# Regrouping the steps of an attention pair by kind, with one more pair in flight

## Chip, core and metric

The kernel runs on one core of one Trainium2 chip. The metric is the device time of an execution in microseconds (us); three runs of the kernel before have a median of 559.45 us (558.18 to 561.83).

The engines are named as in the profile: PE is TensorE's matmuls, PEld its weight loads, DVE is VectorE, ACT is ScalarE, POOL is GpSimd and SP is the queue that issues most DMAs. L491 is line 491 of the kernel.

## What is computed

The reference is blockwise causal attention followed by a mixture of experts with one expert per token:

```python
# attention: B, H, S, D = 8, 8, 576, 64; blocks of 64
scores = scale * q @ k.T                       # per batch and head
scores = where(pos_q // 64 >= pos_k // 64, scores, -1e9)
scores = scores - max(scores, axis=-1)
attn = exp(scores);  attn = attn / (sum(attn) + 1e-9)
x = (attn @ v), heads side by side             # [B, S, 512]
# experts: E = 8, F = 1024
logits = x @ w_gate;  local = sigmoid(x @ w_local)
for each batch, for s in order:                # a scan over the tokens
    e = argmax(logits[s]) if s == 0 or local[s] < 0.5 else e of token s - 1
    out[s] = softmax(logits[s])[e] * (relu(x[s] @ w1[e]) @ w2[e])
```

## The kernel before

**Pairs.** Attention works on 32 pairs of heads (NPR = 32; four pairs are one batch). A pair's queries and keys come in by DMA in their natural layout (`load_qk`, tile `natb`, two buffers), are turned by eight 128x128 transposes into the PSUM tile `ps_t` (L742), and are copied by ACT into `plb` (L747, L748; two buffers). The last 64 tokens, the tail, go through one more transpose (L775) and two small copies (L792, L793). From `plb` DVE makes rounded copies `kh` (keys, L749) and `qd` (queries laid out block-diagonally, L751); POOL adds their tails (L795, L797).

**Maxima.** `top` computes each query block's scores roughly from `kh` and `qd` in three jobs (L464, L470), and DVE takes the row maxima (L474 to L480). `shift` lets POOL spread their negatives into `diag`.

**Scores.** The exact scores are made in four segments (`SEGS`). `products` (L491) multiplies keys and queries in fp32, the two heads on separate halves of TensorE's rows; `less` (L499) adds the negative maxima from `diag` into the same PSUM tile `ps_s`; `expo` (L509) lets ACT write the exponentials to `prob`, and POOL clears the masked corners (L514).

**Products with V.** `av` (L522, L530) multiplies `prob` by V with a column of ones; `norm` (L438, L439) divides by the sums on DVE. `turn_x` and `turn_x_tail` (L536, L542) transpose the result x for the gate, `store_x` writes it to DRAM as bf16, and after every second pair `gate_sums` (L555, L561) adds up the gate's logits.

**PSUM.** The jobs' tiles, `ps_t` and `ps_s` share one pool of two buffers (`ps_sp`, 2 banks each); one more tile of two banks (`ps_mp`) serves jobs 1 and 2; `g0` and `g1` have a bank each.

**The loop.** The program's order on every engine is the order written out by hand. In pass `it` four pairs are in work: a = it + 2 (turned, maxima of jobs 0 and 1), c = it + 1 (maxima of job 2, then scores), e = it (products with V) and x = it - 1 (turned for the gate, stored). The order within a pass is: loads; job 2 of c and its `shift`; norm and store of x; Q/K transposes of a; score segments 0 and 1 of c, interleaved; turning x and the tail of a; jobs 0 and 1 of a; tail of x; part of e's products with V; score segments 2 and 3 of c; the rest of `shift`; the expert weights' DMA for one slice (`load_weights`); the rest of e's products with V; gate sums.

**Routing work** is hung into passes by a table `plan` with places "begin", "turn", "mid" and "end". In passes 9, 17 and 25 `fresh` and `fresh_b` find each token's own best expert (with one ACT exponential, L162) and `to_rows` lays the choice out in rows; one pass later `scan_rows` scans them; two passes later `chosen_ps` and `chosen` fetch the result and `ranks_ps` starts the ranks; three passes later `ranks`, `ranks_b` and `shares` finish. Passes 29 and 30 plan the experts' tiles (`plan1`, `high`, `low`, `inverse`).

After pass 31 the experts' phase runs 38 tiles of 128 tokens, with the last quarter's routing between them. It uses the memory of `natb` and `plb` for the current expert's first weights (`w1c`).

Of the kernel before, what the change touches and what calls it, by code (L numbers as in the profile page):

```python
# [16 lines left out]
def kernel(  # L17
# [11 lines left out]
    nc = tc.nc  # L29
    F32 = mybir.dt.float32  # L30
# [15 lines left out]
    P = 128  # L46
# [43 lines left out]
    def rt(shape, dt, name):  # L90
# [46 lines left out]
    natb = rt([P, 2, 9, 2, D], F32, "natb")  # L137
    plb = rt([P, 2, 2 * S + 64], F32, "plb")
    w1c = [t[:, 0:WE] for t in (natb.rearrange("p z t h d -> p (z t h d)").bitcast(BF16),
                                plb.rearrange("p z n -> p (z n)").bitcast(BF16))]  # L140
# [233 lines left out]
    with tc.manual_schedule():  # L374
# [25 lines left out]
        def load_qk(i, eng=nc.sync):  # L400

            b, hp = divmod(i, HP)
            t = natb[:, i % 2]
            for w, src in enumerate((q, k)):
                s = src[b, 2 * hp:2 * hp + 2]
                for h in range(2):
                    eng.dma_start(out=t[:, 4 * w:4 * w + 4, h, :],
                                  in_=s[h, :512].rearrange("(so si) d -> si so d", si=128))
                eng.dma_start(out=t[64 * w:64 * w + 64, 8],
                              in_=s[:, 512:S].rearrange("h p d -> p h d"))  # L410
            nats[i] = t

# [90 lines left out]
        def seg_tile():  # L503
            return ps_sp.tile([P, 2, 512], F32, tag="s", name="ps_s")

# [39 lines left out]
        def keep_x(x, g0, g1):  # L545
            xTs[x] = o_p.tile([P, S], F32, tag="xT", name="xT")
            nc.scalar.copy(xTs[x][:, 0:512], g0)
            nc.scalar.copy(xTs[x][:, 512:576], g1[:, 256:320])
# [104 lines left out]


        load_qk(0)
        load_qk(1, nc.scalar)
        nc.sync.dma_start(out=wgl[:, :, :E],
# [5 lines left out]
        def scr_f(a, n):  # L663
# [8 lines left out]
        nat_bf = natb.rearrange("p z t h d -> p (z t h d)").bitcast(BF16)  # L672
        ohl1 = nat_bf[:, 0:n1 * P].rearrange("p (c t) -> p c t", t=P)
        rhs1 = nat_bf[:, n1 * P:n1 * (P + 2 * NT1)].rearrange("p (c j t) -> p c j t",
                                                              j=2, t=NT1)
# [4 lines left out]
        tmpt1 = scr_f(2312, NT1 * E)[0:1].rearrange("p (t e) -> p t e", e=E)  # L680

# [34 lines left out]
        for it in range(-2, NPR):  # L716
            a, c, e, x = it + 2, it + 1, it, it - 1
            on_a, on_c, on_e, on_x = (0 <= y < NPR for y in (a, c, e, x))
            if it >= -1 and 1 <= a and a + 1 < NPR:
                load_qk(a + 1)  # L720
            if on_c:
                load_v(c)

            if on_c:
                top(c, 2, ps_mp)
                shift(c, 2, 2)
                shift(c, 8, 1)
            if on_x:
                norm(x, g0_b, 0, 6)
                store_x(x)  # L730
# [6 lines left out]
            if on_a:  # L737
                nat = nats[a]
                ps = ps_sp.tile([P, 2, 512], F32, tag="s", name="ps_t")
                for w in (1, 0):  # L740
                    for t in range(4):
                        nc.tensor.transpose(ps[:, w, 128 * t:128 * t + 128],  # L742
                                            nat[:, 4 * w + t].rearrange("p h d -> p (h d)"),
                                            id_f)
                pl = pls[a] = plb[:, a % 2]
                mxs[a] = o_p.tile([P, 9], F32, tag="mx", name="mx")
                nc.scalar.copy(pl[:, S:S + 512], ps[:, 1, :])  # L747
                nc.scalar.copy(pl[:, 0:512], ps[:, 0, :])  # L748
                nc.vector.tensor_copy(kh[:, 0:512], pl[:, S:S + 512])  # L749
# [5 lines left out]
            if on_c:  # L755
                ps0, ps1 = seg_tile(), seg_tile()
                products(c, ps0, 0, 0)
                products(c, ps1, 1, 0)
                less(ps0, 0, 0)
                products(c, ps0, 0, 1)  # L760
                less(ps0, 0, 1)
                expo(c, ps0, 0)
                less(ps1, 1, 0)
                products(c, ps1, 1, 1)
                less(ps1, 1, 1)
                expo(c, ps1, 1)

            b_done = (x - 1) // HP if on_x and x >= 1 and (x - 1) % HP == HP - 1 else None
            if on_a or on_e or on_x:
                g1 = g_tile(1)  # L770
            if on_x:
                g0 = g_tile(0)
                turn_x(x, g0)
            if on_a:
                nc.tensor.transpose(g1[:, 384:512],  # L775
                                    nat[:, 8].rearrange("p h d -> p (h d)"), id_f)
            if b_done is not None:
                turn_sums(b_done, g1)
            run(it, "turn", g1)
            if on_a:  # L780
                top(a, 0, ps_sp)
                top(a, 1, ps_mp)
            if on_x:
                turn_x_tail(x, g1)
            if on_e:
                xs[e] = o_p.tile([P, 9, D], F32, tag="x", name="x", bufs=1)
                av(e, g1, 4)
                av(e, g1, 3)
            if on_x:
                keep_x(x, g0, g1)  # L790
            if on_a:
                nc.scalar.copy(pl[:, 512:576], g1[:, 384:448])  # L792
                nc.scalar.copy(pl[:, 2 * S - 64:2 * S + 64].rearrange("p (a t) -> p a t", a=2),  # L793
                               g1[:, None, 448:512].to_broadcast([P, 2, 64]))
# [5 lines left out]
            if on_e:  # L800
                norm(e, g1, 6, 3)
            run(it, "mid", g1)

            if on_c:
                for z in (2, 3):
                    ps = seg_tile()
                    products(c, ps, z, 0)
                    less(ps, z, 0)
                    expo(c, ps, z)
            if on_a:  # L810
                shift(a, 4, 4)
                shift(a, 0, 2)
# [11 lines left out]

            if on_e:
                g0_b = g_tile(0)
                for m in (2, 1, 0):
                    av(e, g0_b, m)
# [30 lines left out]
        def results():  # L859
            cur[0], cur[1] = g_tile(0), g_tile(1)  # L860
            turn_x(x, cur[0])
            turn_x_tail(x, cur[1])
            keep_x(x, cur[0], cur[1])
# [116 lines left out]
```

## Time and profile before

| | us |
|---|---|
| three runs: median (lowest, highest) | 559.45 (558.18, 561.83) |
| the profiled execution | 556.25 |
| its span, first to last instruction | 554.4 |
| start to pass 0 | 26.56 |
| passes 0 to 30 | 362.43 |
| pass 31 and the experts' phase | 165.41 |
| a plain pass, up to its gate sums (it 14) | 11.16 |
| the same with its gate sums, which every second pass has | 11.94 |

The profile is of one execution, with 1.85 us outside its span. Passes are told apart in the PE timeline by the job of four matmuls (L470 x4) that opens each, since everything on PE comes in program order. Rows there are merged: "x4" is four instructions of one line in a row, with the start of the first. A matmul's end is modelled, so the distance between starts says more than the length. Mean granted TensorE clock is 0.994.

### The profile page before, as it was taken

Reading aid. Unit: us, or ns where it says so; the run is one execution under the profiler, and the core shown is the slowest. Engines: PE = TensorE matmul, PEld = TensorE weight load, DVE = VectorE, ACT = ScalarE, POOL = GpSimd, SP = SyncE. Lnnn points to the kernel's source line nnn. Section 1 sums busy time; section 2 is a strip of 40 time slices with the busy share of each in tenths; the row PEclk is TensorE's granted clock in tenths of the full one; section 3 lists DMA queues with packets and bytes.
Section 4 is the critical chain, followed back from the end, with each engine's and each line's share of the span. In section 5 each row is a group of like instructions: output and inputs, shape, how many; then the busy total and the mean of one; then the engine's idle time right before and its main releaser. Section 6 shows DMA issues by size and latency. Waiting matters only on the chain.

```text
span 554.4 us, 18510 instructions
## 1 busy us (share of the span) xinstructions
PE 517.1 (93%) x7327; PEld 398.9 (72%) x7327; DVE 334.3 (60%) x756; ACT 248.3 (45%) x487; POOL 254.6 (46%) x510
## 2 busy tenths in 40 slices
PE   2899999999999999999999999999899989999991
PEld 2567777778777777876777777787777767777770
DVE  2565555655759656566855466699557885444440
ACT  1345444454544454444444444544354544454450
POOL 2343343433453433353333435334668766766752
PEclk9999999999999999999999999999999999999997
DMA  6377766885578977468987638964523323323321
GB/s 121 85 127 140 142 139 124 139 150 115 104 136 146 163 146 141 86 116 148 165 158 128 135 71 138 173 109 74 110 79 105 118 90 108 117 89 111 105 89 52
DMA packets 161060, 66.44 MB, mean 120 GB/s; under 512 B 145076, under 2 KB 153292, under 8 KB 160972
## 3 DMA queue, kind: packets, MB, share of 16 engines
q0 software_dynamic: 17760, 31.79, 28.9%
q1 hardware_dynamic: 140812, 32.83, 28.9%
q8 instruction: 61, 1.00, 0.8%
q10 hardware_dynamic: 2400, 0.59, 0.6%
q14 instruction: 27, 0.22, 0.2%
HBM read 67.48 MB, written 15.00 MB: 149 GB/s over the span
## 4 chain that ended last, share of the span: by engine, by line
PE 72%; DVE 10%; issue 5%; ACT 4%; DMA 3%; POOL 2%; SPq 1%; POOLq 0%; DVEq 0%; ACTq 0%
PE ps_s L491 13%; PE g L530 12%; PE ps_h L628 10%; PE ps_o L640 9%; PE ps_m L470 7%; DVE mx L480 5%; PE ps_m L464 4%; PE ps_s L499 3%; ACT plb L748 3%; PE g L522 3%; PE g L536 3%; PE ps_t L742 2%; PE g L555 1%; PE g L542 1%; PE ps_x L613 1%
## 5 line engine op out<-in xcount | busy, mean ns | idle before, releaser
L491 PE MATMUL ps_s<-plb 64*128 64x320 f32 (+4 forms) x768 | 130.0, 419 | 6.6 <-ACT plb L748 6.6
L509 ACT ACTIVATE prob<-ps_s 128x1024 f32<-128x1024 f32 (+2 forms) x128 | 100.3, 835 | 60.6 <-PE ps_s L499 49.4
L491 PEld LDWEIGHTS ps_s<-plb 64*128 64x128 f32 x768 | 62.9, 187 | 48.2 <-ACT plb L748 29.0
L530 PEld LDWEIGHTS g<-vt,prob 128*64 128x64 f32 x2560 | 79.9, 138 | 9.8 <-issue 9.8
L530 PE MATMUL g<-vt,prob 128*64 128x65 f32 x2560 | 86.9, 223 | 0.0
L480 DVE TENSOR_REDUCE mx<-ps_m 128x1 f32<-128x576 f32 (+2 forms) x96 | 43.3, 506 | 67.7 <-PE ps_m L470 67.7
L483 POOL TENSOR_TENSOR diag<-negi,mx 128x128 bf16<-128x128 f32 (+2 forms) x128 | 52.1, 424 | 59.8 <-DVE rs L438 25.5
L640 PE MATMUL ps_o<-w_bf,hT 128*128 x304 | 71.7, 379 | 0.0
L474 DVE TENSOR_REDUCE mx<-ps_m 128x2 f32<-128x1024 f32 x32 | 39.1, 1223 | 48.1 <-PE ps_m L470 48.1
L514 POOL MEMSET prob<- 64x128 f32 x128 | 23.8, 199 | 89.8 <-ACT prob L509 85.3
L470 PE MATMUL ps_m<-kh,qd 128*128 128x512 f32 (+5 forms) x224 | 56.2, 336 | 2.1 <-DVE mx L477 2.1
L632 ACT ACTIVATE hT<-ps_h 128x512 bf16<-128x512 f32 x76 | 45.4, 598 | 26.3 <-PE ps_h L628 25.9
L499 PE MATMUL ps_s<-diag,ones 64*128 64x320 bf16 (+4 forms) x384 | 48.5, 274 | 1.1 <-POOL diag L483 1.1
L644 ACT ACTIVATE o_sb<-ps_o,share 128x512 f32<-128x512 f32 x38 | 26.1, 688 | 51.1 <-PE ps_o L640 43.0
L640 PEld LDWEIGHTS <-hT 128*128 128x128 bf16 x304 | 28.3, 98 | 27.3
L795 POOL CAST kh<-plb 128x64 fp32r<-128x64 f32 x32 | 7.6, 237 | 84.9 <-issue 76.4
L747 ACT COPY plb<-ps_t 128x512 f32<-128x512 f32 x32 | 18.8, 586 | 62.0 <-PE ps_t L742 62.0
L617 DVE COPY scr<-ps_x 128x512 bf16<-128x512 bf16 x38 | 16.1, 424 | 49.8 <-PE ps_x L613 49.5
L470 PEld LDWEIGHTS ps_m<-kh,qd 128*128 128x128 f32 x224 | 38.1, 193 | 7.6 <-issue 1.8
L742 PE MATMUL ps_t<-id_f,natb 128*128 128x128 f32 x256 | 35.0, 282 | 8.0 <-DMA natb<-in_k_dram 8.0
L628 PEld LDWEIGHTS <-plb 128*128 128x128 bf16 x608 | 35.4, 98 | 5.8 <-DVE plb L608 1.7
L751 DVE CAST qd<-plb 64x512 fp32r<-64x512 f32 x64 | 39.0, 609 | 0.6
(194 smaller groups left out, 865.5 us busy)
## 6 DMA issues: line engine op xcount, KB each, us to landing
w_bf<-in_moe_w_dram POOLq DMA_DIRECT2D x32, 512.0 KB, 6.0
vt<-in_v_dram SPq DMA_DIRECT2D x64, 128.0 KB
natb<-in_q_dram SPq DMA_DIRECT2D x62, 128.0 KB
natb<-in_k_dram SPq DMA_DIRECT2D x62, 128.0 KB
x_rows<-xb SPq DMA_DIRECT2D x32, 128.0 KB
vt<-in_v_dram SPq DMA_DIRECT2D x32, 32.0 KB
x_rows<-xb SPq DMA_DIRECT2D x64, 8.0 KB
natb<-in_q_dram SPq DMA_DIRECT2D x31, 32.0 KB
```

The lines of the kernel that those rows point to most:

```text
L470: nc.tensor.matmul(flat[:, c + k0:c + k0 + nn], lhsT=qd[:, b, :], rhs=kh[:, k0:k0 + nn], start=True, stop=True)
L474: nc.vector.reduce_max(mx[:, 6:8], ps, axis=AX)
L480: nc.vector.reduce_max(mx[:, b:b + 1], flat[:, c:c + n], axis=AX)
L483: nc.gpsimd.tensor_tensor(diag[:, s0:s0 + n, :], negi[:, None, :].to_broadcast([P, n, 64]), mxs[i][:, s0:s0 + n, None].to_broadcast([P, n, ...
L491: nc.tensor.matmul(ps[:, h, c:c + n], lhsT=pls[i][rows(h), S + 128 * j:S + 128 * j + 128], rhs=pls[i][rows(h), a:a + n], start=True, stop= ...
L499: nc.tensor.matmul(ps[:, h, c:c + n], lhsT=ones[rows(h), :], rhs=diag[rows(h), a // 64:(a + n) // 64, :], start=False, stop=True)
L509: nc.scalar.activation(p[:, :, SEG0[s]:SEG0[s] + w], ps[:, :, 0:w], func=AF.Exp, scale=scale_attn)
L530: nc.tensor.matmul(g[rows(e), o + 65 * h:o + 65 * h + 65], lhsT=p[:, h, c:c + 64], rhs=t[:, j, h, :], start=(j == 0), stop=(j == m))
L628: nc.tensor.matmul(ps_h[:, f, :], lhsT=w[:, ko * F + fo * P:ko * F + fo * P + P], rhs=xb[:, ko * P:(ko + 1) * P], start=(ko == 0), stop=(k ...
L632: nc.scalar.activation(hT[:, half * 4:half * 4 + 4, :], ps_h, func=AF.Relu)
L640: nc.tensor.matmul(ps_o, lhsT=hT[:, fo, :], rhs=w2_bf[:, bass.ds(woff + fo * Dm, Dm)], start=(fo == 0), stop=(fo == FO - 1))
L742: nc.tensor.transpose(ps[:, w, 128 * t:128 * t + 128], nat[:, 4 * w + t].rearrange("p h d -> p (h d)"), id_f)
```

## The change

The steps of a pass are regrouped, and a fifth pair is in work: r = it + 3 is turned, a = it + 2 has all three maxima jobs, c = it + 1 all four score segments (in the order 3, 2, 0, 1, one after the other), e and x are as before. The loop starts at -3. The order on PE is: maxima of a; turning x; Q/K transposes and tail of r; scores of c; tail of x; all products with V of e; gate sums.

Turned queries and keys have three buffers. Natural queries and keys have one, which is loaded again once the pair in it has been turned (pair 1's natural data sits in the third turned buffer, which is still unused then). `load_qk` is split: the four large loads, then the two tails (`load_tails`). The bf16 copy of x (`xb`) has one buffer instead of two. On SP the order in a pass is now: the stores of x, the loads of Q/K, the loads of V. On ACT the copy of turned x, the copies of turned Q/K with their tails, and the gate's sums come ahead of all four exponentials.

Routing work moves with it: what was in "mid" is mostly in "turn", ahead of the scores on ACT and DVE; `chosen_ps` has a new place "ahead"; `shares` comes a pass later; `low` in pass 30 is one operation in "begin".

```diff
-    natb = rt([P, 2, 9, 2, D], F32, "natb")
-    plb = rt([P, 2, 2 * S + 64], F32, "plb")
...
+    PLW, NAW = 2 * S + 64, 9 * 2 * D
+    qkb = rt([P, NAW + 3 * PLW], F32, "qkb")
+    plb = [qkb[:, NAW + PLW * i:NAW + PLW * i + PLW] for i in range(3)]
+    qk_bf = qkb.bitcast(BF16)
+    w1c = [qk_bf[:, z:z + WE] for z in (0, 2 * (NAW + PLW))]
...
-            t = natb[:, i % 2]
+            z = NAW + 2 * PLW if i == 1 else 0
+            t = qkb[:, z:z + NAW].rearrange("p (t h d) -> p t h d", h=2, d=D)
...
+        def load_tails(i, eng=nc.sync):
+            b, hp = divmod(i, HP)
+            for w, src in enumerate((q, k)):
+                eng.dma_start(out=nats[i][64 * w:64 * w + 64, 8],
+                              in_=src[b, 2 * hp:2 * hp + 2, 512:S].rearrange("h p d -> p h d"))
...
-            xb = o_p.tile([P, 9, D], BF16, tag="xb", name="xb")
+            xb = o_p.tile([P, 9, D], BF16, tag="xb", name="xb", bufs=1)
...
-            at(i0, "mid", lambda ps, g=g: fresh(g))
-            at(i0, "mid", lambda ps, g=g: fresh_b(g))
+            at(i0, "turn", lambda ps, g=g: fresh(g))
+            at(i0, "turn", lambda ps, g=g: fresh_b(g))
...
-            at(i0 + 1, "mid", lambda ps, g=g: scan_rows(g, buf))
-            at(i0 + 2, "turn", lambda ps, g=g: chosen_ps(g, ps, buf))
-            at(i0 + 2, "mid", lambda ps, g=g: chosen(g, ps))
+            at(i0 + 1, "turn", lambda ps, g=g: scan_rows(g, buf))
+            at(i0 + 2, "ahead", lambda ps, g=g: chosen_ps(g, ps, buf))
+            at(i0 + 2, "turn", lambda ps, g=g: chosen(g, ps))
...
-            at(i0 + 3, "turn", lambda ps, g=g: shares(g))
-            at(i0 + 3, "mid", lambda ps, g=g: ranks(g))
+            at(i0 + 3, "turn", lambda ps, g=g: ranks(g))
             at(i0 + 3, "mid", lambda ps, g=g: ranks_b(g))
+            at(i0 + 4, "turn", lambda ps, g=g: shares(g))
...
-        at(30, "turn", lambda ps: low(ohl1[:, 0:GC, :], 0, GC))
-        at(30, "mid", lambda ps: low(ohl1[:, GC:n1, :], GC, n1 - GC))
+        at(30, "begin", lambda ps: low(ohl1, 0, n1))
```

The loop body after the change:

```python
for it in range(-3, NPR):
    r, a, c, e, x = it + 3, it + 2, it + 1, it, it - 1
    if on_x:
        norm(x, g0_b, 0, 6)
    run(it, "begin", ge)
    ...
    for job, pool in enumerate((ps_sp, ps_sp, ps_mp)):
        if on_a:
            top(a, job, pool)
    ...
    if on_x:
        g0 = g_tile(0)
        turn_x(x, g0)
        store_x(x)
        nc.scalar.copy(xT_of(x)[:, 0:512], g0)
    if on_r:
        ...
        nxt = {0: 2, 1: None}.get(r, r + 1 if r + 1 < NPR else None)
        if nxt is not None:
            load_qk(nxt)
            load_tails(nxt)
    if on_c:
        load_v(c)
    if b_done is not None:
        turn_sums(b_done, g1)
    run(it, "ahead", g1)
    if on_r:
        ...
    if b_done is not None:
        keep_sums(b_done, g1)
    run(it, "turn", g1)
    if on_c:
        for z in (3, 2, 0, 1):
            ps = ps_sp.tile([P, 2, 512], F32, tag="s", name="ps_s")
            for part in range(len(SEGS[z])):
                products(c, ps, z, part)
                less(ps, z, part)
            expo(c, ps, z)
    if on_a:
        shift(a, 0, 5)
        shift(a, 5, 4)
    if -1 <= it < NPR - 1:
        load_weights(it + 1)
    ...
    if on_x:
        turn_x_tail(x, g1)
    if on_e:
        av(e, g1, 4)
        av(e, g1, 3)
    if on_x:
        nc.scalar.copy(xT_of(x)[:, 512:576], g1[:, 256:320])
    if on_e:
        norm(e, g1, 6, 3)
        run(it, "mid", g1)
        g0_b = g_tile(0)
        for m in (2, 1, 0):
            av(e, g0_b, m)
    ...
```

More of the change, by code (lines that the diff above doesn't have):

```diff
@@ L543, in turn_x_tail, with xT_of @@
                                  rhs=id_f[:, rows(h)], start=True, stop=True)
[L545 to L548, printed above, removed]
+        def xT_of(x):
+            if x not in xTs:
+                xTs[x] = o_p.tile([P, S], F32, tag="xT", name="xT")
+            return xTs[x]
         def gate_sums(x, gl):
@@ L671 @@
         n1 = 3 * GC
[L672 to L675, printed above, removed]
+        ohl1 = qk_bf[:, 0:n1 * P].rearrange("p (c t) -> p c t", t=P)
+        rhs1 = qk_bf[:, n1 * P:n1 * (P + 2 * NT1)].rearrange("p (c j t) -> p c j t",
+                                                             j=2, t=NT1)
         ohh1 = scr[:, 0:n1 * NT1].rearrange("p (c t) -> p c t", t=NT1)
@@ L715 @@
         ge = None
[L716 to L727, printed above, removed]
+        for it in range(-3, NPR):
+            r, a, c, e, x = it + 3, it + 2, it + 1, it, it - 1
+            on_r, on_a, on_c, on_e, on_x = (0 <= y < NPR for y in (r, a, c, e, x))
             if on_x:
                 norm(x, g0_b, 0, 6)
-                store_x(x)
             run(it, "begin", ge)
@@ L736 @@
                 first(1)
-            if on_a:
-                nat = nats[a]
+            for job, pool in enumerate((ps_sp, ps_sp, ps_mp)):
+                if on_a:
+                    top(a, job, pool)
+            b_done = (x - 1) // HP if on_x and x >= 1 and (x - 1) % HP == HP - 1 else None
+            if on_r or on_e or on_x:
+                g1 = g_tile(1)
+            if on_x:
+                g0 = g_tile(0)
+                turn_x(x, g0)
+                store_x(x)
+                nc.scalar.copy(xT_of(x)[:, 0:512], g0)
+            if on_r:
+                nat, pl = nats[r], plb[r % 3]
+                pls[r] = pl
+                mxs[r] = o_p.tile([P, 9], F32, tag="mx", name="mx")
                 ps = ps_sp.tile([P, 2, 512], F32, tag="s", name="ps_t")
@@ L753 @@
                         pl[rows(h), 0:512].rearrange("p (b t) -> p b t", t=64))
[L755 to L794, printed above, removed]
                 nc.gpsimd.tensor_copy(kh[:, 512:576], pl[:, 2 * S - 64:2 * S])
@@ L799 @@
                 keep_sums(b_done, g1)
-            if on_e:
-                norm(e, g1, 6, 3)
-            run(it, "mid", g1)
+            run(it, "turn", g1)
             if on_c:
[L805 to L808, printed above, removed]
+                for z in (3, 2, 0, 1):
[3 more added lines that the diff above has]
+                        less(ps, z, part)
                     expo(c, ps, z)
             if on_a:
-                shift(a, 4, 4)
-                shift(a, 0, 2)
+                shift(a, 0, 5)
+                shift(a, 5, 4)
             if -1 <= it < NPR - 1:
@@ L823 @@
                                for i in range(2)]
+            if on_x:
+                turn_x_tail(x, g1)
             if on_e:
+                xs[e] = o_p.tile([P, 9, D], F32, tag="x", name="x", bufs=1)
+                av(e, g1, 4)
+                av(e, g1, 3)
+            if on_x:
+                nc.scalar.copy(xT_of(x)[:, 512:576], g1[:, 256:320])
+            if on_e:
+                norm(e, g1, 6, 3)
+                run(it, "mid", g1)
                 g0_b = g_tile(0)
@@ L862, in results @@
             turn_x_tail(x, cur[1])
-            keep_x(x, cur[0], cur[1])
+            nc.scalar.copy(xT_of(x)[:, 0:512], cur[0])
+            nc.scalar.copy(xT_of(x)[:, 512:576], cur[1][:, 256:320])
         def sums():
```

19 lines of the change are left out of this document (11 added, 8 removed).

## Prediction, made before the changed kernel was run

> **What bounds the kernel now.** I read the page first: its busy times and its chain of work.
>
> ```profile
> PE 517.1 (93%) x7327; PEld 398.9 (72%) x7327; DVE 334.3 (60%) x756; ACT 248.3 (45%) x487; POOL 254.6 (46%) x510
> PE 72%; DVE 10%; issue 5%; ACT 4%; DMA 3%; POOL 2%; SPq 1%; POOLq 0%; DVEq 0%; ACTq 0%
> ```
>
> TensorE carries the chain. Next the windows by stage: attention's passes 0 to 30 run from 26.56 to 388.99 us. Columns: length, then busy time of PE, PEld, DVE, ACT, POOL, then clock, DMA share, GB/s.
>
> ```profile
> 26.56:388.99 362.43, 352.42 (x5404) 275.89 (x5404) 232.11 (x532) 167.11 (x351) 143.48 (x401) 1.00 0.73 131
> ```
>
> PE is idle there for only 10 us of 362. So a gain must come out of what counts as busy. Third, the PE timeline of one plain pass (it 14, no routing work), from 188.97 to its gate sums at 200.13, 11.16 us. First columns: start, length; I use the distance from one start to the next as the true cost.
>
> ```profile
> 188.97 0.83 PE L470 MATMUL ps_m<-kh,qd 128*128 128x512 f32 x4
> 189.63 1.04 PE L742 MATMUL ps_t<-id_f,natb 128*128 128x128 f32 x8
> 190.60 1.02 PE L491 MATMUL ps_s<-plb 64*128 64x448 f32 x4
> 191.84 0.81 PE L491 MATMUL ps_s<-plb 64*128 64x320 f32 x4 [0.21 <-ACT plb L748]
> 192.48 0.36 PE L499 MATMUL ps_s<-diag,ones 64*128 64x448 bf16 x2
> ...
> 193.33 0.25 PE L499 MATMUL ps_s<-diag,ones 64*128 64x192 bf16 x2
> 193.51 0.65 PE L536 MATMUL g<-id_f,x 128*128 128x128 f32 x4
> 194.00 0.27 PE L775 MATMUL g<-id_f,natb 128*128 128x128 f32 x1
> 194.21 0.50 PE L464 MATMUL ps_m<-kh,qd 128*128 128x512 f32 x1
> 194.54 0.39 PE L470 MATMUL ps_m<-kh,qd 128*128 128x512 f32 x1
> ...
> 195.39 0.34 PE L542 MATMUL g<-id_f,x 128*64 128x64 f32 x4
> ...
> 197.17 0.81 PE L491 MATMUL ps_s<-plb 64*128 64x320 f32 x4
> 197.81 0.30 PE L499 MATMUL ps_s<-diag,ones 64*128 64x320 bf16 x2
> 197.95 0.60 PE L491 MATMUL ps_s<-plb 64*128 64x256 f32 x4
> 198.38 0.28 PE L499 MATMUL ps_s<-diag,ones 64*128 64x256 bf16 x2
> 198.59 1.62 PE L530 MATMUL g<-vt,prob 128*64 128x65 f32 x48
> 200.13 0.64 PE L555 MATMUL g<-xT,wgl 128*32 128x128 f32 x16
> ```
>
> Two things are to be seen. (a) Where the tile shape changes, the first weight load is not hidden. Products of 256 columns behind products take 0.43 (197.95 to 198.38), so 64 columns cost 0.107; 320 columns should take 0.53, but behind V's products (128*64) they take 0.64. Likewise subtraction of 320 columns takes 0.14, but that of 256 followed by another shape 0.21. Each change costs about 0.10. (b) The 448 columns should take 0.10 + 0.75, to 191.45, yet the next products start at 191.84: a wait of 0.39 on the copies of the turned queries and keys. Fourth, the ACT timeline of the same pass:
>
> ```profile
> 190.71 0.59 ACT L747 COPY plb<-ps_t 128x512 f32<-128x512 f32 x1 [2.48 <-PE ps_t L742]
> 191.19 0.59 ACT L748 COPY plb<-ps_t 128x512 f32<-128x512 f32 x1
> ```
>
> The first copy starts only after all eight transposes (189.63 + 1.04 = 190.67), and PE gets the buffer 1.17 after that.
>
> **The change, step by step in a plain pass.** No matmul is added or removed; order and waits change. I lay the new order out from S = 0, the first maximum.
> - Maxima, six then four: 1.18 (194.21 to 195.39) and 0.66. One exposed first load goes (the first 512 takes 0.33, the second 0.23 or 0.24), and so does the gap ahead of the next shape (0.20 for the last 128 columns instead of 0.07): 1.64.
> - Turning x: 4 at 0.11 = 0.45, to 2.09. It needs x normalised: DVE's 0.18 + 0.56 after the last V product, done by about 0.9, hidden.
> - Eight Q/K transposes, 0.87 (0.97 less the shape change), and the tail, 0.11, with the change 0.10: to 3.17. They need the first maxima's buffer: DVE's norm, then a reduction of 1.22, done by about 2.1. That is just in time.
> - Segment 3: 0.10 + 0.43 + 0.11, to 3.81.
> - Segment 2 needs the transposes' buffer: 2.09 + 1.04 + 1.17 = 4.30. So the old wait is still there, 0.49 instead of 0.39. Then 0.64 + 0.14, to 5.08.
> - Segment 0 needs segment 3's exponential. On ACT it stands behind both copies and two tail copies (starts 0.10 apart, 0.28 the last), so it starts at 4.48, takes 0.59 (the page by form, 128x512), and frees PE at 5.13. Then 0.10 + 0.75 + 0.19 + 0.17 + 0.03, to 6.37.
> - Segment 1: 0.10 + 0.53 + 0.13 + 0.33 + 0.18, to 7.64. The exponential it needs is over by 6.1.
> - x's tail 0.16 and V's products 0.59 + 1.03 + 1.54: 10.96.
>
> That is 0.20 less than 11.16. Gate sums add 0.78 every second pass before and after.
>
> **What hides the rest.** SP issues 12 DMAs a pass, about 0.4 to 0.65 each. The three stores now go first, then six Q/K loads, which wait for the turn (about 3.2), then V's. Q/K are issued by about 7 and wanted at 13; at the start of the trace two pairs' loads, 0.8 to 7.95, took 7.1 us together. So one buffer suffices, with 3 us to spare; without that cover each us late costs 30. V's loads queue behind them, out by about 9, used in the next pass from 18.9. GpSimd's cast (0.79), tail casts, four memsets and two shifts (one 0.6 to 0.8 each) end by about 11, and the shifts are wanted at 14. The third buffer removes no wait on this path; its cost is nil.
>
> **Passes with routing work.** Moving the fresh-expert step ahead of the scores puts its exponential (ep) ahead of all four score exponentials on ACT. Pass 9 before:
>
> ```profile
> 140.27 0.22 DVE L158 TENSOR_REDUCE sm<-lg_all 128x9 f32<-128x72 f32 x1
> 140.94 0.26 ACT L162 ACTIVATE ep<-ep 128x72 f32<-128x72 f32 x1 [1.26 <-DVE ep L161]
> ```
>
> ACT waits for DVE here, and little hangs on it. After the change DVE must first finish reductions (4.4) and the copies of keys and queries (0.34 and 0.85 to 1.31, to 5.6 or 6.1); ep is ready 0.67 later, segment 3's exponential ends at about 7.1 to 7.5, and segment 0 waits some 2.2 with everything behind it. These passes go from 11.99 to about 13.2: three times +1.2. In the passes that follow the rank step DVE reaches the first reduction 0.3 late, three times: +0.9. The passes that fetch chosen experts took 11.37, 12.10 and 11.38; now 0.11 of their work falls into the wait and the fetch, issued after V's loads, has longer: -1.9. The three passes with sums alone were 11.42, now about 11.05: -1.1.
>
> **Ends.** Before, pass 0 starts at 26.56. The new order does one more transposition and all of pair 1's maxima by then, on a PE that runs at half speed (eight transposes 1.94 at 7.95, 1.04 later), with gaps filled: I take 0, within 1 either way. Pass 0 loses x's work either way, 10.97 to about 10.35: -0.6. Passes 29 and 30 were 11.41 and 11.72. Pass 30 now begins with turning x, which stands behind 2.9 us of planning on DVE: PE waits 2.8, then needs 9.7. Together about 22.35 instead of 23.13: -0.8. The experts' phase (165.4 us) is the same.
>
> [...]
>
> **Sum.** 19 other passes at -0.20: -3.8. Then -1.1 + 3.6 + 0.9 - 1.9 - 0.6 - 0.8 + 0 = +0.1. In all -3.7. The profiled execution took 556.25 (span 554.4), so 552.5; the three runs' median is 559.45, and the same shift gives 555.7. I say 555.5.
>
> **Rivals.**
> - Slower: ScalarE becomes the bound within the scores. All four exponentials now come in one run behind four copies, and segment 0 hangs on the third link. For it: my walk has PE arrive at 5.08 and ACT free it at 5.13, no slack. Against: ACT is busy 167 of 362. Every 0.1 late costs 3 us over 30 passes; from about 0.3 late the kernel is slower. At 0.35 it is 10.5 more, 566.
>  [...]
> - Faster by more: the routing passes do not stall, since DVE and ACT come to them earlier than I walk it. The +3.6 and +0.9 go, and a us at the start: 550.
> - Q/K loads late with one buffer: a landing 10 us after issue would cost 0.5 a pass, over 570. The 7.1 above speaks against.
> - Nothing: the regrouping's 0.20 is an error of reading starts; 559.
>
> **Chances and range.** Forecast (551.5 to 560) 0.42, ScalarE 0.23, no routing stall 0.22, nothing 0.08, late loads 0.05. Over 1% (5.6 us, what a measurement can tell) faster means under 553.9: the 0.22 and 0.12 of the forecast, 0.34. Slower: 0.23 + 0.05 = 0.28. Within: 0.38. The range, 548 to 567, leaves out the late loads and the tails of both sides.
>
> **What would show it.** A plain pass of 10.9 to 11.0; products of 320 columns still waiting about 0.5 on the second copy; in passes 9, 17 and 25 a PE wait of about 2 on ACT; in pass 30 one near 2.8 on DVE. Wrong if plain passes are 11.3 or longer, with PE waiting on the score exponentials or on the first reduction, or if Q/K transposes wait on DMA.

## Result and profile after

The changed kernel takes 579.1 us (median of 4 runs, 578.19 to 584.82) against 560.5 (4 runs) of the kernel before beside it: ratio 1.0358, 95% interval 1.0279 to 1.0436. It is slower by 3.6%. The profiled execution took 578.31, with a span of 576.6; 22.2 more than before is to be accounted for. Lines of the page first (busy times; the chain of work):

```profile
PE 516.5 (90%) x7301; PEld 404.1 (70%) x7327; DVE 318.7 (55%) x755; ACT 255.6 (44%) x487; POOL 236.9 (41%) x446
...
PE 73%; DVE 11%; ACT 5%; DMA 4%; issue 3%; POOL 1%; SPq 1%; DVEq 0%; POOLq 0%; ACTq 0%
```

PE is as busy as before, 517, in a longer span: most of what was added is waiting. The window of passes 0 to 30, now 27.50 to 399.07 (length, PE, PEld, DVE, ACT, POOL, clock, DMA share, GB/s):

```profile
27.50:399.07 371.57, 345.99 (x5392) 276.68 (x5391) 215.54 (x525) 174.28 (x347) 136.07 (x338) 0.98 0.70 129
```

PE idles 26 us there instead of 10, and the clock is 0.98 instead of 1.00. By stage (each pass from its first maximum to that of the next):

| us | before | after | more |
|---|---|---|---|
| start to pass 0 | 26.56 | 27.50 | 0.9 |
| passes 0 to 28 | 339.30 | 347.43 | 8.1 |
| of these: 9, 17, 25 (fresh experts) | 36.03 | 38.48 | 2.4 |
| of these: 11, 19, 27 (chosen experts fetched) | 34.94 | 48.48 | 13.5 |
| of these: the other 23 | 268.33 | 260.47 | -7.9 |
| passes 29 and 30 | 23.13 | 24.14 | 1.0 |
| pass 31 to the second tile's first product | 8.98 | 13.66 | 4.7 |
| the rest | 156.43 | 163.87 | 7.4 |

The plain pass came out as walked, and a little better. The PE timeline of pass 14 (start, length):

```profile
191.28 0.50 PE L471 MATMUL ps_m<-kh,qd 128*128 128x512 f32 x1
...
193.40 1.06 PE L751 MATMUL ps_t<-id_f,qkb 128*128 128x128 f32 x8
...
194.65 0.70 PE L498 MATMUL ps_s<-qkb 64*128 64x256 f32 x4
195.16 0.30 PE L506 MATMUL ps_s<-diag,ones 64*128 64x256 bf16 x2
195.62 0.81 PE L498 MATMUL ps_s<-qkb 64*128 64x320 f32 x4 [0.16 <-ACT qkb L755]
...
196.41 1.02 PE L498 MATMUL ps_s<-qkb 64*128 64x448 f32 x4
...
199.08 0.76 PE L526 MATMUL g<-vt,prob 128*64 128x65 f32 x20
199.66 2.50 PE L534 MATMUL g<-vt,prob 128*64 128x65 f32 x80
202.10 0.64 PE L559 MATMUL g<-xT,wgl 128*32 128x128 f32 x16
```

From 191.28 to 202.10 it is 10.82, against 11.16 before and 10.96 in the walk. Segment 0 starts 5.13 after the first maximum, as walked, and waits for nothing on ACT. Segment 2 starts 0.35 after segment 3's work is through (195.16 + 0.11), where the walk had 0.49 and the kernel before 0.39. The 0.14 that the walk missed is in the products with V: made in one piece they take 3.02 (199.08 to 202.10), and the walk put them at 3.16. What PE waited for in the whole run (total, times, longest):

```profile
PE g L191 <- DMA scr<-e_dram: 10.6, 3, 3.8
PE ps_t L751 <- DMA qkb<-in_k_dram: 7.7, 1, 7.7
PE ps_h L632 <- DVE scr L621: 6.8, 5, 3.1
PE ps_s L498 <- ACT prob L513: 5.5, 3, 1.8
...
PE g L540 <- DVE x L446: 3.2, 1, 3.2
```

Of these the 7.7 is the first load of the kernel, there before as well. The others are new or larger: three fetches of chosen experts (L191), the experts' first products (L632), three score segments behind ACT (L498), and x's turning in pass 30 (L540).

**The fetch.** The timeline of passes 9 to 11 of the changed kernel, all engines. L64 is `load_weights`; L181 writes the layout of the expert choice to DRAM and L182 reads it back; L187 writes the scanned row and L188 reads it; L191 is `chosen_ps`.

```profile
140.75 0.80 POOL L64 DMA_DIRECT2D w_bf<-in_moe_w_dram  x1
141.60 0.36 SPq L181 DMA_DIRECT2D a_dram<-scr  x1
145.70 0.26 SPq L182 DMA_DIRECT2D scr<-a_dram  x1
...
151.57 0.81 POOL L64 DMA_DIRECT2D w_bf<-in_moe_w_dram  x1
154.95 0.40 SPq L187 DMA_DIRECT2D e_dram<-scr  x1
158.52 0.30 SPq L188 DMA_DIRECT2D scr<-e_dram  x1
...
159.89 0.17 PE L191 MATMUL g<-id_b,scr 9*128 9x9 bf16 x1 [3.25 <-DMA scr<-e_dram]
```

The same in the kernel before:

```profile
142.81 0.37 SPq L180 DMA_DIRECT2D a_dram<-scr  x1
143.04 0.80 POOL L64 DMA_DIRECT2D w_bf<-in_moe_w_dram  x1
144.10 0.26 SPq L181 DMA_DIRECT2D scr<-a_dram  x1
153.74 0.39 SPq L186 DMA_DIRECT2D e_dram<-scr  x1
154.20 0.80 POOL L64 DMA_DIRECT2D w_bf<-in_moe_w_dram  x1
155.01 0.29 SPq L187 DMA_DIRECT2D scr<-e_dram  x1
```

A read is issued when its write has landed: in the changed kernel SP waits on `a_dram` ahead of L182 three times, 11.0 in all, and on `e_dram` ahead of L188 three times, 9.9 in all. Before, in all three groups, each small write went out 0.02 to 0.6 us ahead of a 512 KB weight transfer and its read followed 1.2 to 1.3 later. Now the weights go first. The write of the layout follows 0.85 later and its read waits 3.9 to 4.2; the write of the scanned row follows 2.7 to 3.4 later and its read waits 3.6 to 3.9. The fetch also stands earlier in the pass, right ahead of the scores, so PE stops there; then the granted clock is one half for 3.4 us (at 160.0; at 255.5, for 6.8; at 354.5). The first of these as a window (length, PE, PEld, DVE, ACT, POOL, clock, DMA share, GB/s):

```profile
160.00:163.40 3.40, 3.40 (x17) 2.06 (x18) 0.40 (x2) 1.52 (x4) 0.73 (x3) 0.50 0.55 120
```

**Pass 31.** POOL (L596: the gathers; L432: the cast in `store_x`), DVE and PE of the changed kernel:

```profile
400.44 1.78 POOL L596 DMA_INDIRECT scr<-x_rows,tok  x1 [4.25 <-DVE tok L335]
402.53 1.62 POOL L596 DMA_INDIRECT scr<-x_rows,tok  x1 [0.30 <-issue]
404.46 0.99 POOL L596 DMA_INDIRECT scr<-x_rows,tok  x1 [0.30 <-issue]
405.50 0.66 POOL L432 CAST xb<-x 128x576 bf16<-128x576 f32 x1
...
406.19 0.36 DVE L446 TENSOR_TENSOR x<-g,rs 128x192 f32<-128x192 f32 x1 [2.86 <-POOL xb L432]
...
407.63 1.12 PE L632 MATMUL ps_h<-scr,qkb 128*128 128x128 bf16 x9 [3.15 <-DVE scr L621]
```

`store_x` now stands behind the three gathers on GpSimd. The tile `x` has one buffer, so DVE cannot normalise pair 31 until the cast of pair 30 has read it; DVE's copy for the first tile stands behind that, and PE behind the copy.

### The profile page after: what moved, and what is told of

Read it like the earlier page. It is cut to its first block, busy times and chain, and to the rows that moved or that the text cites. A ratio compares the mean times of both kernels' runs of the same rounds, so it can differ in the third digit from the quotient of the medians.

```text
span 576.6 us, 18266 instructions
## 1 busy us (share of the span) xinstructions
PE 516.5 (90%) x7301; PEld 404.1 (70%) x7327; DVE 318.7 (55%) x755; ACT 255.6 (44%) x487; POOL 236.9 (41%) x446
## 4 chain that ended last, share of the span: by engine, by line
PE 73%; DVE 11%; ACT 5%; DMA 4%; issue 3%; POOL 1%; SPq 1%; DVEq 0%; POOLq 0%; ACTq 0%
PE ps_s L498 16%; PE ps_h L632 12%; PE g L534 11%; PE ps_o L644 10%; PE ps_m L477 4%; PE ps_s L506 3%; PE ps_t L751 3%; DVE mx L481 3%; PE g L526 3%; PE ps_m L471 2%; ACT qkb L754 2%; ACT qkb L755 2%; DVE mx L483 2%; DMA e_dram<-scr 2%; PE ps_x L617 2%
## 5 line engine op out<-in xcount | busy, mean ns | idle before, releaser
L498 PE MATMUL ps_s<-qkb 64*128 64x320 f32 (+4 forms) x768 | 132.7, 439 | 10.5 <-ACT prob L513 5.5
L513 ACT ACTIVATE prob<-ps_s 128x1024 f32<-128x1024 f32 (+2 forms) x128 | 107.9, 845 | 40.2 <-PE ps_s L506 36.2
L498 PEld LDWEIGHTS ps_s<-qkb 64*128 64x128 f32 x768 | 64.8, 196 | 51.9 <-ACT prob L513 16.4
L632 PEld LDWEIGHTS <-qkb 128*128 128x128 bf16 x1216 | 72.4, 99 | 19.0 <-issue 10.9
L445 DVE RECIPROCAL rs<-g 128x3 f32<-128x3 f32 x64 | 12.0, 187 | 129.9 <-ACT xT L812 111.9
L632 PE MATMUL ps_h<-scr,qkb 128*128 128x128 bf16 x1216 | 75.5, 221 | 7.1 <-DVE scr L621 6.8
L776 POOL CAST kh<-qkb 128x64 fp32r<-128x64 f32 x32 | 8.3, 259 | 122.6 <-ACT qkb L769 111.3
L743 ACT COPY xT<-g 128x512 f32<-128x512 f32 x31 | 18.2, 586 | 80.8 <-PE g L540 80.8
L612 DVE COPY qkb<-w_bf 128x4096 bf16 x40 | 48.9, 1225 | 8.3 <-PE ps_h L632 3.5
L621 DVE COPY scr<-ps_x 128x512 bf16<-128x512 bf16 x38 | 16.1, 423 | 57.2 <-PE ps_x L617 49.6
L751 PE MATMUL ps_t<-id_f,qkb 128*128 128x128 f32 x256 | 36.2, 288 | 7.7 <-DMA qkb<-in_k_dram 7.7
```

The source lines that it names most:

```text
L498: nc.tensor.matmul(ps[:, h, c:c + n], lhsT=pls[i][rows(h), S + 128 * j:S + 128 * j + 128], rhs=pls[i][rows(h), a:a + n], start=True, stop= ...
L513: nc.scalar.activation(p[:, :, SEG0[s]:SEG0[s] + w], ps[:, :, 0:w], func=AF.Exp, scale=scale_attn)
L612: nc.vector.tensor_copy(w, w1_bf[:, bass.ds(off, WE)])
L632: nc.tensor.matmul(ps_h[:, f, :], lhsT=w[:, ko * F + fo * P:ko * F + fo * P + P], rhs=xb[:, ko * P:(ko + 1) * P], start=(ko == 0), stop=(k ...
L751: nc.tensor.transpose(ps[:, w, 128 * t:128 * t + 128], nat[:, 4 * w + t].rearrange("p h d -> p (h d)"), id_f)
```

## The experiments

Twelve kernels, each timed against the kernel before on its own chip (whose median was 559.2, 558.9, 555.6 and 558.6 in the four sessions), so ratios are what compares. Edits are to the changed kernel unless said otherwise.

**1. Chosen experts fetched among the products with V.**

```diff
-            at(i0 + 2, "ahead", lambda ps, g=g: chosen_ps(g, ps, buf))
-            at(i0 + 2, "turn", lambda ps, g=g: chosen(g, ps))
+            at(i0 + 2, "mid", lambda ps, g=g: chosen_ps(g, ps, buf))
+            at(i0 + 2, "mid", lambda ps, g=g: chosen(g, ps))
```

> The changed kernel with one edit: the matmul that fetches the chosen experts and the DVE step behind it go from ahead of the scores to the place among the products with V, in passes 11, 19 and 27. Theory A (the row of chosen experts lands too late for the new place; the wait of 3 us on it and the half clock that follows are the whole of the +14 us in these passes): passes 11, 19 and 27 come back from 16.1, 16.9 and 15.7 to about 11 to 11.5, no PE wait on the chosen row is left, no half clock at 160, 256 and 355 us, and the whole goes from 579 to about 565. Theory B (these passes are long for another reason, one buffer for natural Q/K that comes late behind the blocked DMA queue): the wait turns up in another line of the same passes, and the time stays within 5 us of 579.

Measured: 570.2 us, ratio 1.0178 (1.0114 to 1.0241). Passes 11, 19 and 27 took 12.3 each, but passes 20 and 28 took 14.0 instead of 11.7: about half of the loss came back. The wait on the chosen row is gone, with its half clock (the 48 products with V behind the fetch take 1.62, as in pass 14 of the kernel before), but the fetch now waits 1.1 behind DVE's normalisation, and in passes 20 and 28 the Q/K transposes came 2.2 late, in the second by the trace for their loads, which SP issues behind the blocked read of the small row. Theory A holds for the wait and theory B for a remainder. Two of the three fresh-expert passes were longer than in the changed kernel, 14.4 instead of 12.8; that comes below.

**2. x 30 stored ahead of the gathers in pass 31.**

```diff
                 norm(x, g0_b, 0, 6)
+                if it == NPR - 1:
+                    store_x(x)
             run(it, "begin", ge)
...
                 turn_x(x, g0)
-                store_x(x)
+                if it < NPR - 1:
+                    store_x(x)
```

> The changed kernel with one edit: in pass 31 the cast and store of x 30 go ahead of the three gathers on GpSimd and SP, as in the kernel before. Theory A (DVE's normalisation of pair 31 waits for that cast, which stands behind the gathers; PE then waits 3.2 us and gets half clock): the stretch from the start of pass 31 to the second tile's first matmul goes from 13.7 back to about 9 us, -4.7 us. Whether the rest of the experts' phase, 7.4 us longer than before, follows is open: if its 0.18 a tile comes from the same late start, it goes too and the total is -8 to -12; if it comes from how DVE and GpSimd get into each other's way, it may stay. Theory B (the experts' phase is late because the routing of the last quarter is): no change beyond 1 us.

Measured: 571.59, ratio 1.0207 (1.0173 to 1.0240). In the trace PE waits 0.52 instead of 3.15 ahead of the first tile's products, no half clock follows, and the first two tiles are 4.9 us shorter:

```profile
404.26 1.95 PE L632 MATMUL ps_h<-scr,qkb 128*128 128x128 bf16 x32 [0.52 <-DVE share L622]
```

The tiles after it still fall behind those of the kernel before, from 9.1 us late at the second to 14.4 at the last. Theory A for pass 31; the loss in the later tiles is another matter.

**3. No weight transfer near the small writes.**

```diff
-            if -1 <= it < NPR - 1:
+            if -1 <= it < NPR - 1 and it not in (9, 10, 17, 18, 25, 26):
                 load_weights(it + 1)
+                if it + 3 in (9, 10, 17, 18, 25, 26):
+                    load_weights(it + 4)
```

> The changed kernel with one edit: the six expert-weight transfers (512 KB each) of passes 9, 10, 17, 18, 25 and 26 are issued three passes earlier, so that none is in flight when the small rows of chosen experts are written to DRAM. Theory A (a small write issued just behind such a transfer waits for it in the DMA engines): the write of the expert choice lands in about 1.3 us instead of 4.1, the write of the scanned row in 1.3 to 2.5 instead of 3.6 (V's loads are still ahead of it), PE's waits on the chosen row fall from 3.2 to 3.8 to about 1 or none, with no half clock behind them, and the time falls by 6 to 12 us. Theory B (the writes land late because of the stores and Q/K and V loads of the same queue): the landings stay at 3.5 to 4, and the time within 3 us.

Measured: 569.6, ratio 1.0196 (1.0162 to 1.0230). The same rows of its timeline:

```profile
144.18 0.36 SPq L181 DMA_DIRECT2D a_dram<-scr  x1
145.44 0.26 SPq L182 DMA_DIRECT2D scr<-a_dram  x1
153.82 0.40 SPq L187 DMA_DIRECT2D e_dram<-scr  x1
155.35 0.30 SPq L188 DMA_DIRECT2D scr<-e_dram  x1
```

1.26 instead of 4.10, and 1.53 instead of 3.57; stores, Q/K and V loads are where they were. PE waits for no fetch, and passes 11, 19 and 27 take 10.9 each: all of the 13.5 us is back, with the fetch still ahead of the scores. Theory A. Part of it was paid elsewhere: with two transfers in one pass V's loads came late (a PE wait of 2.4), and passes 8 and 16 took 14.3 instead of 11.6. In pass 25 the Q/K loads came 2.1 late, and it took 14.6 instead of 12.8.

**4. Four edits at once**: 1 and 2, the fresh-expert step (all of it) back in "mid", and `plan1` in pass 28 "mid" with `plan1_b` in pass 29 "turn".

> The changed kernel with four edits: the chosen experts fetched among the products with V, x 30 stored ahead of the gathers, the fresh-expert step (with its exponential) back among the products with V, and the experts' planning half a pass earlier, so that DVE is free for the normalisation ahead of pass 30. If the regrouping itself is a gain of 0.3 us a pass, as the plain passes say, and the rest is what these four places cost: -14 -5 -3 (three times 0.8 to 1.2) -3 to -4 (a wait of 3.2 and its half clock) = about -25, 554, which would be about 1% under the kernel before (560); with the 7 us of the experts' phase back too, 548. If the time stays above 565, most of the loss lies elsewhere.

Measured: 560.99 (nine runs, 556.04 to 564.16), ratio 1.0020 (0.9985 to 1.0055): no faster than before, some 7 us over the estimate. Three places show why. Fresh-expert passes went to 12.47 only, since the layout of the choice now waited 1.4 on DVE. Fetch passes took 12.3 each and the passes behind them 12.5, 13.4 and 14.8 instead of 11.7: the small writes still landed late, and the Q/K loads of pass 28, issued behind one of them, kept PE waiting 1.96, with half clock behind it (four products of 256 columns take 1.23 instead of 0.70). That is the cost of one buffer for natural Q/K, hidden in the changed kernel by the longer wait for the fetch. And the tiles drifted as in experiment 2.

**5. Weight transfers of those six passes behind the tail casts of the next pass.**

```diff
+            if -1 <= it < NPR - 1 and it not in (9, 10, 17, 18, 25, 26):
                 load_weights(it + 1)
...
                     nc.gpsimd.tensor_copy(qd[rows(h), 8, rows(h)], pl[rows(h), 512:576])
+                if it - 1 in (9, 10, 17, 18, 25, 26):
+                    load_weights(it)
```

> The changed kernel with one edit: in passes 9, 10, 17, 18, 25 and 26 the expert-weight transfer (512 KB) is issued on GpSimd not at the end of the pass but in the next pass behind the tail casts, some 5 us later, so behind the small write in time and never twice in one pass. Theory A (a small write lands only once the weight transfer ahead of it is through): as with the transfers moved three passes ahead, passes 11, 19 and 27 take 11.1 to 11.6 instead of 15.8 to 17.0, but passes 8 and 16 stay at 11.57 (they took 14.3 with two transfers in one pass): 563 to 566, about -14. Theory B (it was the total of transfers in flight, not their order): the waits on the chosen row come back at over 2 us.

Measured: 563.91, ratio 1.0088 (1.0060 to 1.0116). Passes 11, 19 and 27: 11.1, 11.5, 11.4; passes 8 and 16: 11.6. PE's waits on the fetch fell from 10.6 in all to 1.8. The write of the layout lands in 1.2 to 1.3 again. That of the scanned row, with a transfer 5.2 to 6.7 us ahead of it, still takes 1.8 to 3.1. Theory A, and the largest single share of the loss: 1.0358 to 1.0088 by the order of six transfers.

**6. Only the fresh experts' exponential behind the scores.**

```diff
-        nc.scalar.activation(ep9, ep9, func=AF.Exp)
+    def fresh_exp():
+        nc.scalar.activation(ep9, ep9, func=AF.Exp)
...
             at(i0, "turn", lambda ps, g=g: fresh_b(g))
+            at(i0, "mid", lambda ps: fresh_exp())
```

> The changed kernel with one edit: of the fresh-expert step only its exponential on ACT goes back behind the four score exponentials; its DVE part stays ahead of the scores. Theory A (the exponential that waits 1.56 us on DVE at the head of ACT's queue is the stall of passes 9, 17 and 25): PE's wait of 1.8 us on the score exponential goes, these passes take about 11.0 instead of 12.8 (and never 14.4, which is the same wait with half clock behind it): -5.5 us, 573. Theory B (DVE itself is the bound of these passes): they stay over 12 us, with a wait on DVE in place of ACT.

Measured: 570.92, ratio 1.0224 (1.0197 to 1.0250). Passes 9, 17 and 25 take 11.0 each instead of 12.8, PE's wait on ACT is gone: theory A, -5.4 us. In the changed kernel, ACT and PE of pass 9 (L163 is that exponential, at the head of ACT's queue):

```profile
134.52 0.26 ACT L163 ACTIVATE ep<-ep 128x72 f32<-128x72 f32 x1 [1.56 <-DVE ep L162]
...
135.32 1.02 PE L498 MATMUL ps_s<-qkb 64*128 64x448 f32 x4 [1.82 <-ACT prob L513]
```

and the same PE step in experiment 1:

```profile
134.78 1.86 PE L498 MATMUL ps_s<-qkb 64*128 64x448 f32 x4 [1.82 <-ACT prob L513]
```

One wait of 1.82, twice; behind the second the matmuls take 1.86 instead of 1.02, at half clock. So it cost 1.8 there and 3.4 here.

**7. Planning earlier.**

```diff
-            at(i0 + 4, "turn", lambda ps, g=g: shares(g))
-        at(29, "turn", lambda ps: plan1(tmpt1))
-        at(29, "mid", lambda ps: plan1_b(tmp1, t1k1, hi1))
+            at(i0 + 4 + (g == 2), "turn", lambda ps, g=g: shares(g))
+        at(28, "turn", lambda ps: plan1(tmpt1))
+        at(29, "turn", lambda ps: plan1_b(tmp1, t1k1, hi1))
```

> The changed kernel with one edit: the experts' planning (DVE) goes from passes 29 to passes 28 and 29 ahead of the scores, and the last group's shares one pass later, into pass 30. Theory A (PE's wait of 3.2 us in pass 30 is the planning that DVE has ahead of the normalisation, and the half clock of 3.4 us behind it comes from that gap): the wait falls under 0.5, the half clock at 389 us goes, pass 30 is 4 to 5 us shorter. Theory B (the wait stays 1 us or more, because DVE has no room in pass 29 either): 1 to 2 us are won.

Measured: 574.79, ratio 1.0289 (1.0250 to 1.0328). The wait in pass 30 is 0.98 instead of 3.17 and the half clock behind it is gone (four products of 256 columns take 0.70 there instead of 1.11); from the start of pass 29 to the gate sums of pass 30 it is 19.5 instead of 22.2. But the first gather now starts 1.3 later behind the table of tokens it reads: the shares' store, a pass later, is what it waits for. Between the two theories.

**8. Five edits**: 2, 5, 6 and 7, and the fetch (`chosen_ps` and `chosen`) in a new place between the scores and x's tail.

> The changed kernel with five edits together: weight transfers of six passes behind the small writes, the chosen experts fetched behind the scores (ahead of x's tail), the fresh-expert exponential behind the scores' own, the planning earlier, x 30 stored ahead of the gathers. If the regrouping is a gain of 0.3 us in plain passes and the losses are these five, then -15 -5.5 -4.5 -5 (pass 31) = -30 from 579: 549, with a spread of 3 us up for the cadence of the experts' tiles; that is 1 to 2% below the kernel before. If it is 559 or more, the regrouping gains nothing that lasts.

Measured: 551.54, ratio 0.9872 (0.9839 to 0.9905): 1.3% under the kernel before. All fetch passes take 11.4, fresh-expert passes 11.0. Passes 0 to 28 are 11.7 us shorter than in the kernel before, 0.34 in a plain pass and 1.0 in each fresh-expert pass. The start takes 1.9 of that (pass 0 begins at 28.47), and the first tile starts 9.7 ahead. Then the tiles lose 5.5 of it. The timeline of one tile, first of the kernel before (POOL L645: the scatter of results, L592: the next gather; DVE L617: the copy of a tile's turned rows):

```profile
486.49 1.01 POOL L645 DMA_INDIRECT out_dram<-o_sb,tok2s  x1 [0.81 <-ACT o_sb L644]
...
487.06 0.39 PE L613 MATMUL ps_x<-id_b,scr 128*128 128x128 bf16 x4
...
487.49 0.43 DVE L617 COPY scr<-ps_x 128x512 bf16<-128x512 bf16 x1 [1.93 <-PE ps_x L613]
487.81 1.61 POOL L592 DMA_INDIRECT scr<-x_rows,tok2g  x1 [0.31 <-PE ps_x L613]
```

then of the changed kernel (L649, L617, L596 and L621 are the same steps):

```profile
505.02 1.01 POOL L649 DMA_INDIRECT out_dram<-o_sb,tok2s  x1 [1.58 <-DVE qkb L612]
...
505.46 0.39 PE L617 MATMUL ps_x<-id_b,scr 128*128 128x128 bf16 x4
506.34 1.02 POOL L596 DMA_INDIRECT scr<-x_rows,tok2g  x1 [0.31 <-PE ps_x L617]
...
507.11 0.42 DVE L621 COPY scr<-ps_x 128x512 bf16<-128x512 bf16 x1 [2.09 <-PE ps_x L617]
```

Before, the copy starts 0.04 after the end of PE's transposes (487.06 + 0.39), which is also where the scatter ends. After, it starts 1.26 after their end, 0.77 into the gather, and PE's next products with it. Both rows name the transposes as what ended DVE's wait; since a matmul's end is modelled, the rows do not tell whether their completion or DVE came late. From tile 20 on every tile repeats its pattern, 3.74 us before and about 3.92 after.

**9. As 8, with that copy on ACT** (`nc.scalar.copy(xb, ps_x)`).

> The version with five edits (551.5), and one more: in the experts' phase the copy of a tile's turned rows out of PSUM goes from DVE to ACT. Theory A (the 0.13 to 0.18 us a tile that the changed kernel loses from tile 18 on is that copy, held back on DVE while GpSimd prepares its gather): the cadence of the tiles is 3.74 us throughout, as in the kernel before, PE's waits on DVE ahead of the experts' first product go, and the whole is 547 to 548. Theory B (the tiles are slower for another reason, GpSimd's or the DMA's): the cadence stays at 3.87 or ACT's later exits make it longer, and the time stays at 551 or above.

Measured: 547.56, ratio 0.9857 (0.9823 to 0.9892). Tiles take 3.74 from the 17th to the last but two, and nothing drifts: theory A for the cadence. For the time the interval overlaps that of experiment 8.

**10. As 9, with the last group's shares back in pass 29.**

> As the one before, with the last group's shares back in pass 29 (ahead of the scores). With the shares in pass 30, the normalisation there came 2 us later, the store of x 30 with it, and the first gather waited for that store: PE waited 3.2 us on the first tile's rows against 0.9 in the version with four edits. Expected: that wait back at about 1, PE's wait in pass 30 up from 1.0 to about 1.4, so about 2 us less than the run beside it, 545 to 546. Rival: the gather waits for the place of the tokens from DVE all the same, and nothing is won.

Measured: 543.42 (542.86 to 544.23), ratio 0.9786 (0.9769 to 0.9803), the best version: 12.2 us under the kernel before on the same chip, 4.1 under the run beside it. The first tile waits 1.3 on its rows instead of 3.2, and the mean granted clock of the profiled execution is 0.991 instead of 0.987. The busy times of its page:

```profile
PE 503.8 (93%) x7301; PEld 397.7 (74%) x7327; DVE 307.0 (57%) x717; ACT 273.4 (51%) x525; POOL 249.0 (46%) x446
```

**11. The kernel before with the copy on ACT.**

> The kernel before with that one edit (the copy of a tile's turned rows on ACT). Its tiles run at 3.74 us from tile 18 on already, which is what its matmuls alone take, so nothing is to be won there; the earlier tiles, with routing work on DVE between them, lose some 2 to 3 us that may partly go. Expected 556 to 559.5. If it came to 552 or less, most of what the five edits and the regrouping won over the kernel before would be this copy's.

Measured: 555.93, ratio 1.0002 (0.9985 to 1.0018). Nothing for the kernel before.

**12. As 10, with the copy back on DVE.**

> The version that has the five edits, the shares in pass 29 and the copy on ACT, with that copy back on DVE: against it only the copy differs. Theory A (the copy on DVE costs the tiles 2 to 5 us here, though the same change did nothing for the kernel before): the ratio to the kernel before is 0.983 to 0.988 instead of 0.979, and the trace has tiles of 3.8 to 3.9 us. Theory B (the gain was the shares' alone, as the small gain of the copy by itself, 0.9857 against 0.9872, would have it): 0.979 to 0.981, and tiles of 3.74 us or a few that are longer.

Measured: 549.34, ratio 0.9836 (0.9795 to 0.9878). Its trace loses 5.1 us on the kernel before between the second tile and the last, where 10 gains 1.0. Theory A by the trace; the two intervals still overlap, by 0.0008.

## Why the prediction was wrong, step by step

Right: the plain pass. Its gain was walked as 0.20 and is 0.34; the other 23 of passes 0 to 28 together won 7.9. Pass 0 won none of its 0.6 (10.95 against 10.97). The mechanism of the fresh-expert stall was right too, with its place and the engine: ACT behind DVE, a PE wait of about 2 at segment 0 (1.8). It cost 2.4 where +3.6 stood. The wait in pass 30 was forecast as 2.8 on DVE and was 3.2. ScalarE as the bound, the rival on the other side, did not come: no plain pass waits on a score exponential.

Wrong, by weight:
- "now 0.11 of their work falls into the wait and the fetch, issued after V's loads, has longer: -1.9". It was +13.5, so 15.4 of the 26 us between forecast and result (-3.7 and +22.2 in the profiled executions). The sentence took the landing of the small writes from before, 1.3, as given. It was so short because they went out 0.02 to 0.6 ahead of the weights on another queue; moving SP's and GpSimd's work turned that order round (experiments 3 and 5). The place of the wait on PE was not weighed either: `chosen_ps` stood at 5.3 after the pass's first maximum and stands at 3.2 where nothing delays it (experiment 3), so there was less time for it, not longer.
- "The experts' phase (165.4 us) is the same." It is 12.1 longer. The edit list of that phase shows nothing, but the loop's last pass runs into it: `store_x` moved past the gathers on GpSimd (4.9, experiment 2), a queue that the walk of pass 31 did not follow. The tiles are the rest: 5.8 between the second and the last, about half of it in the repeating pattern from tile 20 on, and 1.6 behind the last. Experiments 9 and 12 put the 5.8 on DVE's copy. The 1.6 stays open: that stretch took 16.9 before, 18.5 in the changed kernel, and 18.2 in experiment 11, which is not regrouped.
- Half clock, for which the sum has no term. In the changed kernel it came five times between pass 11 and the first tiles: the granted clock is 0.50 in the windows 160:161, 256:257, 355:356, 389:390 and 406:407, each time beside a PE wait of 3.15 to 3.76, which it overlaps or follows within 1 us. Behind pass 30 it is one of the two terms that made 1.0 out of -0.8. In fresh-expert passes it cost 1.5 a time (12.83 without it in pass 9 of the changed kernel, 14.36 with it in that of experiment 1), behind waits of 1.8.
- The prologue, put at 0 within 1, was +0.9, within its bound.
- "So one buffer suffices, with 3 us to spare": true in plain passes, and wrong in the passes with a blocked SP queue, where Q/K landed up to 2.2 us late once nothing else held PE (experiments 1 and 4).

The range missed mainly because it had no case in which a DMA other than Q/K lands late, so nothing in it priced the small rows: without their 15.4 the result would be 563.7, inside the range. Not settled: what keeps DVE's copy waiting in the slower cadence. The traces show the gather running at that time, but put the wait down to PE's transposes; the order of scatter and gather was not tried. Nor was it tried what sets the kernel into the one cadence or the other. Of the edits to the changed kernel only the copy was tried on the kernel before, so it is not shown that all of the 2% is the regrouping's.

## What to carry to other kernels

When steps are reordered, list for each small DRAM round trip what bulk transfer stands ahead of it on any queue, before and after; a landing time in a trace belongs to that order and not to the transfer (here 4.10 us and 1.26 for the same 4.5 KB). Follow each moved call to the last pass of the loop, and see which other calls it passes there on each queue. A gain of 0.3 us a pass was real here, and the kernel came out 2% ahead only once six places, none of them in a plain pass, had been put back or moved apart.

## What the hardware showed

- A write of 4.5 KB on SP's queue landed, by the issue of its read, 1.2 to 1.3 us after its own issue with no weight transfer shortly ahead of it (the kernel before, experiments 3 and 5). It took 3.9 to 4.2 in the changed kernel, where 512 KB had been issued on GpSimd's queue 0.85 earlier. Experiment 3 takes only the other queue's transfers away from there, and 4.10 became 1.26: a transfer on another queue held the write back. By what means, no run shows.
- Waits of PE of the same length had two prices. The 1.8 us wait in fresh-expert passes was followed by half clock in 3 of 15 passes (the changed kernel and experiments 1, 2, 5 and 7); waits of 3.25 to 4.00 on the fetch in 11 of 12 (the changed kernel and experiments 2, 6 and 7). Behind the fetch of the changed kernel the granted clock was 0.50; in the experiments it is read from the matmuls' length (four of 256 columns 1.22 instead of 0.70). The episodes last 3.4 us or 6.8.
- In the tiles that repeat, DVE's copy out of PSUM started 0.03 to 0.04 us after the end of PE's transposes before, and 1.24 to 1.28 after it in the changed kernel, 0.75 to 0.79 into a gather. In earlier tiles it also started 0.3 to 0.4 into a gather or a scatter. In the tiles that repeat, the gather took 1.6 where a DVE copy of 4096 elements fell into it and 1.02 where not, also with the copy out of PSUM inside it. What makes it longer, no run here separates.
